# A two-filter spectral kernel: another bank plan and order for its last two stages, and another order of one step's products

## The chip, the cores and the metric

The kernel runs on one core of a Trainium2 chip. The metric is the device time of one execution in microseconds. The five engines of the core work through queues of their own: TensorE (PE in the profile; PEld is its weight loads), VectorE (DVE), ScalarE (ACT), GpSimd (POOL) and SyncE (SP), which issues most of the DMA transfers. They meet only at semaphores.

## The reference

`x` is 2048 x 1024 in bfloat16. Two filters A and B each take the two-dimensional real FFT of `x`, multiply it by a complex weight and transform it back; a sigmoid gate, one number for each row, mixes the two results.

```
x = A_x
g = _sigmoid((x * gate_w).sum(-1, keepdims=True))
X = rfft2(x)
a = irfft2(X * (A_w_r + 1j * A_w_i)).astype(bfloat16)
b = irfft2(X * (B_w_r + 1j * B_w_i)).astype(bfloat16)
return g * a + (1 - g) * b
```

Both filters read the same `x`, so the forward transform is done once.

## The kernel before

All transforms are products with constant matrices on TensorE, and the kernel keeps everything in SBUF. The numbering of the stages is that of the code.

*Stages 1 to 4* make the spectrum. After stage 1 they run as 16 **steps** `i` (`step`, line 643): stage 4 of step `i` is four matmuls (line 477) into two PSUM banks, and ScalarE copies them (line 485) into one of seven buffers in the tile XF. Step `i` uses buffer `(i + 1) % 7`, so step 14 overwrites the buffer of step 7, and step 15 that of step 8. A DMA (`swap`, line 487) writes the same data with real and imaginary parts exchanged into a second buffer in the tile MM.

*Products.* VectorE multiplies the spectrum of a step by the weights (`product`, line 493; the instruction is line 504). A step has four kinds: A0 and B0 write into the rows of the other half, A1 and B1 then write over rows that A0 and B0 read. A kinds read the direct buffer (XF), B kinds the swapped one (MM). The table `ORDER` (lines 656 to 660) gives by hand which products VectorE is handed after which step. For steps 7 and 8 each kind is cut into a first half of columns (`lo7`, `lo8`) and a second half (`up7`, `up8`). **These steps 7 and 8 are not stage 7 below.** Every dependency inside VectorE is also a semaphore wait: in this program only TensorE's instructions are never made to wait for earlier ones of the same engine.

*Stage 5* (line 600) transforms back along one axis in 32 groups of 16 matmuls, each into one of four pairs of banks, each copied by ScalarE (line 611) or now and then VectorE (line 609). Groups 1 to 15 and 0 read the products of steps 0, 1, 2 and 4 to 8, groups 16 to 31 those of steps 3 and 9 to 15. The last two groups, 30 and 31, leave banks 2 to 5.

*Stage 6* (line 748) and *stage 7* (line 777) run for 16 **row blocks** `r`. `stage6_mm(r)` is 32 small matmuls into a pair of banks, and `stage6(r)` copies the pair (line 759 on VectorE for half of block 0, line 761 on ScalarE for the rest). `stage7(r)` multiplies that by the constants DI and DJ and ends in one of three ways:

- *folded* (the `else` branch): 8 matmuls of 256 columns; ScalarE copies one bank (line 784), VectorE adds and subtracts (line 824), and GpSimd makes the output with two more (line 829);
- *half unfolded* (`HALF`): 4 matmuls of 256 and 4 of 512; ScalarE copies 256 columns, VectorE does two small additions (line 810) and two large ones that make the output (line 788). GpSimd has nothing to do;
- *wholly unfolded* (`FULL`): 8 matmuls of 512; ScalarE copies 512 columns, VectorE makes the output with line 788 alone. Block 15 ends in four additions of half the size.

Stage 7 takes banks 4 and 5 for even blocks and 2 and 3 for odd ones, so a block reuses the banks of the block two before it, and must wait until VectorE has read them. Stage 6 takes banks 0 and 1 for even blocks, 6 and 7 for odd ones. The loop (line 847) hands TensorE the stage 6 of two blocks (a "pair") ahead of the stage 7 of every odd block from 1 to 13: pair 2 and 3 before block 1, and so on. The eviction of the pair's first block goes before ScalarE's copy of this stage 7, the second one after it.

The store of a block is issued by SyncE as soon as its output is there, in the order of the blocks up to 12. Then come block 14 on ScalarE's queue, half of block 15 on SyncE's, block 13 on SyncE's, and the other half of block 15 on ScalarE's. The output tiles are reused after six blocks, GpSimd's input buffers after four folded blocks.

Of the kernel before, what the change touches and what calls it, by code (L numbers as in the profile page):

```python
# [232 lines left out]
def bass_gated_mix__spectral_gfnet__spectral_gfnet__prompt_kernel(nc, A_x, A_w_r, A_w_i, B_x, B_w_r, B_w_i, gate_w, out):  # L233
# [25 lines left out]
    def sl(t, off, dims, p0=0, np_=128, pstep=1):  # L259
        n = t.shape[1]  # L260
        return AP(t, p0 * n + off, [[n * pstep, np_]] + [list(x) for x in dims])

    def ps(col, dims):
        return AP(PS, col, [[4096, 128]] + [list(x) for x in dims])

    def bank(b):
        return ("ps", b)
# [28 lines left out]
    for _ in range(18):  # L296
        P.add("pe", lambda e: e.matmul(ps(7 * 512, [(1, 256)]), sl(CL, GRo, [(1, 128)]), sl(CL, GRo, [(1, 256)]), start=True, stop=True),
              r=["GRz"], w=[bank(7)])
# [354 lines left out]
    rest = lambda i, *a: tuple((i, k) + a for k in ("A0", "B0", "A1", "B1"))  # L653
    each = lambda *a: lambda kinds: tuple((a[0], kinds[k:k + 2]) + a[1:] for k in range(0, len(kinds), 2))
    rest = lambda *a: each(*a)("A0B0A1B1")
    ORDER = (((0, "A0"),), ((1, "A0"),), (), ((3, "A0"), (2, "A0")), ((0, "B0"), (4, "A0"), (0, "A1")))
    ORDER += tuple(((k + 1, "B0"), (k, "B1"), (k + 1, "A1")) for k in range(4))
    ORDER += tuple(((k, "A0"), (k, "B0"), (k - 1, "B1"), (k, "A1")) for k in (5, 6))
    lo7, lo8, up7, up8 = (each(k, c, 1) for c in range(2) for k in (7, 8))
    ORDER += (lo7("A0B0") + ((6, "B1"),) + lo7("A1"), lo7("B1") + lo8("A0B0A1B1") + up7("A0B0") + up8("A0B0") + up7("A1") + up8("A1") + up7("B1") + up8("B1"), rest(9))  # L660

    def products(i):
        for a in ORDER[i]:
# [70 lines left out]
    Yo = lambda k, r: (8 * k + r // 2) * RP + 264 + r % 2 * 128  # L734
    OUT = [(MM, 1024 * k) for k in range(4)] + [(XF, 6144 + 1024 * k) for k in range(2)]

    def stage6_mm(r, bs, pis):
        b0 = 6 * (r % 2)
        t6, o6, _ = RBS[r]
        for b in bs:  # L740
            for pi in pis:
                for cp in range(2):
                    n = cp * 64 + 16 * b + r
                    for h in range(2):
                        lh = sl(W, n * RP + pi, [(2, 128)], p0=64 * h, np_=64)
                        rh = sl(t6, o6 + cp * 256 + b * 32, [(128, 2), (1, 32)], p0=64 * h, np_=64)
                        o = ps((b0 + h) * 512 + pi * 256 + b * 32, [(128, 2), (1, 32)])
                        P.add("pe", lambda e, o=o, lh=lh, rh=rh, cp=cp: e.matmul(o, lh, rh, start=(cp == 0), stop=(cp == 1)),  # L748
                              r=[("Z", pi), ("RB", r)], w=[bank(b0 + h)])

    def stage6(r):
        b0 = 6 * (r % 2)
        for k in range(2 if r == 0 else 1):
            n = 4 if r == 0 else 8
            src = ps((b0 + k) * 512, [(128, n), (1, 32), (32, 4)])
            dst = sl(W, Yo(4 * k, r), [(8 * RP, n), (4, 32), (1, 4)])
            kw = dict(r=[bank(b0 + k + q) for q in range(n // 4)], a=[("Y", r)], after=[last5])
            if r == k == 0:
                P.add("dve", lambda e, s=src, d=dst: e.tensor_copy(d, s), **kw)
            else:  # L760
                P.add("act", lambda e, s=src, d=dst: e.activation(d, s, ACT.Copy), **kw)  # L761

    HALF, FULL = (2, 7, 10, 13), (5, 14, 15)
    pqc = 0

    def stage7(r):
        nonlocal pqc
        full, half = r in FULL, r in HALF
        b0 = 6 * (r - 14) if r >= 14 else 4 - 2 * (r % 2)
        ot, oo = OUT[r % NOU]  # L770
        eo = 4096 + r % 2 * 1024
        es = sl(XF, eo, [(1, 1024)]).bitcast(f32)

        def mm(col, c0, n, ri, pi, h, k, last):
            lh = sl(W, Yo((1 - h) * 4 + pi * 2 + ri, r), [(1, 128)])
            rh = sl(FT, DIo + pi * 2048 + (ri * 2 + h) * 256 + c0 * 4096, [(4096, n), (1, 256)])
            P.add("pe", lambda e: e.matmul(ps(col, [(1, n * 256)]), lh, rh, start=(k == 0), stop=(k == last)),  # L777
                  r=[("Y", r), "DI"] + ["DJ"] * (full or half), w=[bank(col // 512)])

        def ods(s, k, n):  # L780
            return sl(ot, oo + 1023 * s + 512 * (1 - 2 * s) * k, [(512 * (1 - 2 * s), n), (1 - 2 * s, 256)])

        def even(c0, n):
            P.add("act", lambda e: e.activation(es[:, :n], ps((b0 + 1) * 512 + c0, [(1, n)]), ACT.Copy), r=[bank(b0 + 1)], w=[("EO", r % 2)], after=[last5])  # L784

        def finals(k0, n, bk, t, o, keys):
            for s, op in enumerate((ALU.add, ALU.subtract)):
                P.add("dve", lambda e, s=s, op=op: e.tensor_tensor(  # L788
                    out=ods(s, k0, n), in0=ps(bk * 512, [(256, n), (1, 256)]),
                    in1=sl(t, o + 512 * k0, [(1, 512 * n)]).bitcast(f32).rearrange("p (a b) -> p a b", a=n), op=op),  # L790
                    r=keys + [bank(bk)], w=[("OU", r % NOU, s, k) for k in range(k0, k0 + n)], after=[last5])

        if full:
            for k in range(4):
                mm((b0 + 1) * 512, 0, 2, 1, k // 2, k % 2, k, 3)
            even(0, 512)
            for k0, n, bk in ((0, 2, b0),) if r < 15 else ((0, 1, b0), (1, 1, 4)):
                for k in range(4):
                    mm(bk * 512, k0, n, 0, k // 2, k % 2, k, 3)
                finals(k0, n, bk, XF, eo, [("EO", r % 2)])  # L800
        elif half:
            for e_ in (1, 0):
                for k in range(2):
                    mm((b0 + 1) * 512 + e_ * 256, 0, 1, 1, k, k ^ e_, k, 1)
            even(256, 256)
            for k in range(4):
                mm(b0 * 512, 0, 2, 0, k // 2, k % 2, k, 3)
            to = 4096 + (r % 2) * 1024
            for s, op in enumerate((ALU.add, ALU.subtract)):
                P.add("dve", lambda e, s=s, op=op: e.tensor_tensor(out=sl(MM, to + s * 512, [(1, 512)]).bitcast(f32),  # L810
                                                                   in0=ps((b0 + 1) * 512, [(1, 256)]), in1=es[:, :256], op=op),
                      r=[("EO", r % 2), bank(b0 + 1)], w=[("T", r % 2, s), ("XS", 4), ("XS", 5)])
            finals(0, 2, b0, MM, to, [("T", r % 2, 0), ("T", r % 2, 1)])
        else:
            for e_ in (1, 0):
                for ri in range(2):
                    for k in range(2):
                        mm((b0 + e_) * 512 + ri * 256, 0, 1, ri, k, k ^ e_, k, 1)
            even(0, 512)
            pk = pqc % NPQ  # L820
            pqc += 1
            pq = pk * 4096
            for s, op in enumerate((ALU.add, ALU.subtract)):
                P.add("dve", lambda e, s=s, op=op: e.tensor_tensor(out=sl(FT, pq + s * 2048, [(1, 1024)]).bitcast(f32), in0=ps(b0 * 512, [(1, 512)]),  # L824
                                                                   in1=es, op=op),
                      r=[("EO", r % 2), bank(b0)], w=[("PQ", pk, s)], after=[last5])
            pv = sl(FT, pq, [(2048, 2), (1, 1024)]).bitcast(f32).rearrange("p a (b c) -> p a b c", b=2)
            for s, op in enumerate((ALU.add, ALU.subtract)):
                P.add("pool", lambda e, s=s, op=op: e.tensor_tensor(out=ods(s, 0, 2), in0=pv[:, :, 0, :], in1=pv[:, :, 1, :], op=op),  # L829
                      r=[("PQ", pk, 0), ("PQ", pk, 1)], w=[("OU", r % NOU, s, k) for k in range(2)])  # L830
        full2 = lambda a: a.rearrange("p (a b) -> p a b", b=256)[:, ::3, :]
        ou = lambda ks: [("OU", r % NOU, s, k) for s in range(2) for k in ks]
        store = lambda eng, name, dst, src, ks: lambda: dma(eng, name, dst, src, r=ou(ks))
        if r < 15:
            return [store("act" if r == 14 else "sp", f"o{r}", outv[:, r, :], sl(ot, oo, [(1, 1024)]), (0, 1))]
        return [store("sp", "o15a", full2(outv[:, r, :]), sl(ot, oo, [(768, 2), (1, 256)]), (0,)),
                store("act", "o15b", outv[:, r, 256:768], sl(ot, oo + 256, [(1, 512)]), (1,))]
# [6 lines left out]
    stage6_mm(1, range(2, 4), (0,))  # L844
    stage6_mm(1, range(4), (1,))
    stage6(1)
    for r in range(16):
        pair = (r + 1, r + 2) if r % 2 and r < 14 else ()
        for q in pair:
            stage6_mm(q, range(4), range(2))  # L850
        for q in pair[:1]:
            stage6(q)
        late += stage7(r)
        for q in pair[1:]:
            stage6(q)
        if r < 13:
            outs.append(late.pop()())
# [63 lines left out]
```

## Time and profile before

| what | value |
|---|---|
| three runs | 121.32, 121.32, 121.65 us; median 121.32 |
| profiled execution | 121.57 us, its span 119.4 us |
| TensorE matmul busy | 110.0 us (92%) |
| TensorE weight loads busy | 88.2 us (74%) |
| VectorE busy | 97.4 us (82%) |
| ScalarE busy | 98.8 us (83%) |
| GpSimd busy | 33.9 us (28%) |
| HBM | 17.48 MB read, 4.19 MB written |

The span runs from the first to the last instruction of the program; the time of an execution has some 2 us more around it. In rows of the timeline the first number is the start in microseconds from the beginning of the span, the second the time from there to the end of the last of the instructions that the row merges; behind them stand engine, line, operation, tiles and shapes, and in brackets the idle time of the engine before the row and what ended it. Consecutive instructions of an engine overlap: a matmul of 256 columns is shown with about 0.27 us, and the next one starts about 0.11 us later. So work in a queue is counted from start to start, not by durations.

### The profile page before, as it was taken

Reading aid. Unit: us, or ns where it says so; the run is one execution under the profiler, and the core shown is the slowest. Engines: PE = TensorE matmul, PEld = TensorE weight load, DVE = VectorE, ACT = ScalarE, POOL = GpSimd, SP = SyncE. Lnnn points to the kernel's source line nnn. Section 1 sums busy time; section 2 is a strip of 40 time slices with the busy share of each in tenths; the row PEclk is TensorE's granted clock in tenths of the full one; section 3 lists DMA queues with packets and bytes.
Section 4 is the critical chain, followed back from the end, with each engine's and each line's share of the span. In section 5 each row is a group of like instructions: output and inputs, shape, how many; then the busy total and the mean of one; then the engine's idle time right before and its main releaser. Section 6 shows DMA issues by size and latency. Waiting matters only on the chain.

```text
span 119.4 us, 4238 instructions
## 1 busy us (share of the span) xinstructions
PE 110.0 (92%) x1812; PEld 88.2 (74%) x1812; DVE 97.4 (82%) x202; ACT 98.8 (83%) x119; POOL 33.9 (28%) x43
## 2 busy tenths in 40 slices
PE   6789999999999999889999999999889899999950
PEld 4566889887665766378999999999877667877420
DVE  0478998985999999999999997994537868999980
ACT  4239998999799999849999999996878968889720
POOL 1000030026664600000000000000006979789940
PEclk9999999999999999999999999999999999999999
DMA  2999999999999999844599800000000242442546
GB/s 89 314 347 412 422 379 354 350 348 349 366 362 371 361 364 363 315 150 144 128 328 401 294 4 5 0 0 5 0 5 0 96 181 88 181 176 93 206 173 236
DMA packets 17683, 26.14 MB, mean 219 GB/s; under 512 B 2113, under 2 KB 11073, under 8 KB 17665
## 3 DMA queue, kind: packets, MB, share of 16 engines
q1 hardware_dynamic: 16368, 23.00, 55.3%
q0 software_dynamic: 864, 2.36, 5.4%
q10 hardware_dynamic: 432, 0.52, 1.3%
q8 instruction: 14, 0.23, 0.8%
q14 instruction: 5, 0.03, 0.1%
HBM read 17.48 MB, written 4.19 MB: 182 GB/s over the span
## 4 chain that ended last, share of the span: by engine, by line
PE 30%; SPq 28%; POOL 12%; DMA 8%; DVE 8%; issue 6%; ACT 3%; POOLq 1%; DVEq 0%; ACTq 0%
SPq L284 28%; PE PS L600 25%; POOL MM L829 9%; DMA W<-in_B_w_i_dram 5%; DMA W<-in_A_x_dram 3%; POOL XF L829 3%; DVE W L504 3%; DVE FT L824 2%; PE PS L380 2%; DVE MM L788 2%; POOLq L860 1%; PE PS L748 1%; PE PS L777 1%; PE PS L477 1%; ACT XF L485 1%
## 5 line engine op out<-in xcount | busy, mean ns | idle before, releaser
L600 PE MATMUL PS<-CL,W 128*128 128x128 bf16 x512 | 32.4, 225 | 0.3 <-DVE W L504 0.2
L600 PEld LDWEIGHTS PS<-CL,W 128*128 128x128 bf16 x512 | 31.7, 145 | 1.3 <-DVE W L504 0.9
L829 POOL TENSOR_TENSOR MM<-FT 128x512 bf16<-128x512 f32 x14 | 17.5, 1277 | 50.9 <-DVE FT L824 50.9
L611 ACT ACTIVATE W<-PS 128x1024 bf16<-128x1024 f32 (+1 forms) x30 | 28.5, 1036 | 1.2 <-PE PS L600 1.1
L504 DVE TENSOR_TENSOR W<-XF,W 128x1024 bf16<-128x1024 bf16 (+2 forms) x36 | 22.1, 631 | 1.3 <-ACT XF L485 1.1
L504 DVE TENSOR_TENSOR W<-MM,W 128x1024 bf16<-128x1024 bf16 (+2 forms) x36 | 22.0, 636 | 0.4 <-DMA MM<-XF 0.2
L777 PE MATMUL PS<-FT,W 128*128 128x256 bf16 (+1 forms) x132 | 20.0, 302 | 0.9 <-DVE MM L788 0.4
L761 ACT ACTIVATE W<-PS 128x1024 bf16<-128x1024 f32 (+1 forms) x16 | 15.8, 994 | 3.5 <-PE PS L748 3.3
L477 PE MATMUL PS<-XF,CK 128*128 128x512 bf16 (+1 forms) x72 | 17.5, 357 | 0.8 <-ACT XF L485 0.8
L485 ACT ACTIVATE XF<-PS 128x1024 bf16<-128x1024 f32 x15 | 16.2, 1078 | 2.5 <-DVE W L504 2.1
L466 ACT ACTIVATE XF<-PS 128x1024 bf16<-128x1024 f32 x16 | 17.1, 1076 | 0.6 <-PE PS L460 0.5
L777 PEld LDWEIGHTS PS<-FT,W 128*128 128x128 bf16 x132 | 12.1, 98 | 6.7 <-DVE MM L788 0.7
L341 DVE TENSOR_TENSOR XF<-W 128x512 bf16<-128x512 bf16 (+2 forms) x34 | 11.4, 403 | 6.2 <-DMA W<-in_A_x_dram 5.9
L380 PE MATMUL PS<-MM,XF 128*128 128x256 bf16 x128 | 14.9, 273 | 1.5 <-DVE XF L341 1.4
L380 PEld LDWEIGHTS PS<-MM,XF 128*128 128x128 bf16 x128 | 12.2, 98 | 4.2 <-DVE XF L341 2.7
L391 ACT ACTIVATE FT<-PS 128x1024 bf16<-128x1024 f32 (+2 forms) x15 | 13.1, 1012 | 0.9 <-PE PS L380 0.9
L284 POOL DMA_DIRECT2D MM<-XF x18 | 9.9, 551 | 13.7 <-PE PS L477 8.1
L824 DVE TENSOR_TENSOR FT<-PS,XF 128x512 f32<-128x512 f32 x18 | 11.5, 683 | 2.3 <-ACT XF L784 2.1
L451 PEld LDWEIGHTS PS<-F,FT 128*128 128x128 bf16 x128 | 8.4, 98 | 3.1 <-ACT FT L391 0.2
L784 ACT ACTIVATE XF<-PS 128x512 f32<-128x512 f32 (+1 forms) x16 | 8.8, 547 | 1.9 <-PE PS L777 1.9
L451 PE MATMUL PS<-F,FT 128*128 128x128 bf16 x128 | 10.2, 219 | 0.0
L477 PEld LDWEIGHTS PS<-XF,CK 128*128 128x128 bf16 x72 | 4.8, 97 | 6.5 <-ACT XF L485 5.4
(63 smaller groups left out, 100.4 us busy)
## 6 DMA issues: line engine op xcount, KB each, us to landing
W<-in_A_x_dram SPq DMA_DIRECT2D x7, 512.0 KB, 7.6
out_dram<-MM SPq DMA_DIRECT2D x10, 256.0 KB, 2.7
MM<-XF POOLq DMA_DIRECT2D x18, 128.0 KB, 5.3
FT<-c_U SPq DMA_DIRECT2D x1, 2048.0 KB, 9.5
MM<-XF SPq DMA_DIRECT2D x14, 128.0 KB, 2.5
W<-in_A_w_r_dram SPq DMA_DIRECT2D x4, 256.5 KB, 6.1
W<-in_A_w_i_dram SPq DMA_DIRECT2D x4, 256.5 KB, 6.6
W<-in_B_w_r_dram SPq DMA_DIRECT2D x4, 256.5 KB, 7.0
```

The lines of the kernel that those rows point to most:

```text
L284: return P.add(eng, lambda e: e.dma_start(dst, src), dma=name, **kw)
L380: P.add("pe", lambda e, o=o, lh=lh, rh=rh, s=s: e.matmul(o, lh, rh, start=(s == 0), stop=(s == 1)), r=[("xf", c % 2, q, h, s ^ j), ("M", c ...
L451: P.add("pe", lambda e, o=o, cs=cs, j=j, t=t, rh=rh: e.matmul(o, fblock(1 + cs, j, t), rh, start=(j == 0), stop=(j == 1)), r=[("F1a" if p ...
L466: P.add("act", lambda e: e.activation(dst, src, ACT.Copy), **kw)
L477: P.add("pe", lambda e, o=o, kind=kind, pm=pm, m=m, rh=rh: e.matmul(o, sl(CK, fbo(kind, pm, m), [(1, 128)]), rh, start=(m == 0), stop=(m = ...
L485: P.add("act", lambda e: e.activation(dst, src, ACT.Copy), **kw)
L504: P.add("dve", lambda e: e.tensor_tensor(out=rows((1 - h) * 64 * RP + sw * HW), in0=sl(xt, xo + 128 * h + 64 * h0, [(0, 2), (256, 4 * ni), ...
L600: P.add("pe", lambda e, o=o, l0=l0, ab=ab: e.matmul(o, sl(W, HW * ab + l0, [(RP, 128)]), sl(CL, KIo[ab], [(1, 128)]), start=(ab == 0), sto ...
L611: P.add("act", lambda e: e.activation(dst, src, ACT.Copy), r=b, a=keys)
L761: P.add("act", lambda e, s=src, d=dst: e.activation(d, s, ACT.Copy), **kw)
L777: P.add("pe", lambda e: e.matmul(ps(col, [(1, n * 256)]), lh, rh, start=(k == 0), stop=(k == last)), r=[("Y", r), "DI"] + ["DJ"] * (full o ...
L829: P.add("pool", lambda e, s=s, op=op: e.tensor_tensor(out=ods(s, 0, 2), in0=pv[:, :, 0, :], in1=pv[:, :, 1, :], op=op), r=[("PQ", pk, 0), ...
```

## The change

Three things, all in the order of the work, its banks, and the choice of branch; the mathematics stays.

1. In the table of products, the direct product A1 of step 7's second halves is handed out right after A0 and B0 of that step, ahead of A0, B0 and A1 of step 8's second halves.
2. Stage 6 of row block 2 moves in front of the loop, in banks 4 and 5, and is copied by VectorE. The pairs then go 3 and 4 before block 2, 5 and 6 before block 4, up to 13 and 14 before block 12, and block 15 alone before block 14. Stage 6 takes banks 0 and 1 for block 0, 4 and 5 for the other even blocks, 6 and 7 for odd ones; stage 7 takes 2 and 3 for even blocks, 0 and 1 for odd ones, with 4 and 5 for block 14, and 6, 7 and 2 for block 15.
3. `HALF` becomes 2, 5, 8, 11, 13 (it was 2, 7, 10, 13), `FULL` 14 and 15 (it was 5, 14, 15). Nine blocks are folded before and after: 0, 1, 3, 4, 6, 8, 9, 11, 12 before, and 0, 1, 3, 4, 6, 7, 9, 10, 12 after.

```diff
@@ -657,7 +657,7 @@
-    ORDER += (lo7("A0B0") + ((6, "B1"),) + lo7("A1"), lo7("B1") + lo8("A0B0A1B1") + up7("A0B0") + up8("A0B0") + up7("A1") + up8("A1") + up7("B1") + up8("B1"), rest(9))
+    ORDER += (lo7("A0B0") + ((6, "B1"),) + lo7("A1"), lo7("B1") + lo8("A0B0A1B1") + up7("A0B0A1") + up8("A0B0A1") + up7("B1") + up8("B1"), rest(9))
@@ -734,8 +734,10 @@
+    S6B = lambda r: 6 if r % 2 else 4 * (r > 0)
+
     def stage6_mm(r, bs, pis):
-        b0 = 6 * (r % 2)
+        b0 = S6B(r)
@@ -749,24 +751,24 @@
     def stage6(r):
-        b0 = 6 * (r % 2)
+        b0 = S6B(r)
...
-            if r == k == 0:
+            if k == 0 and r in (0, 2):
                 P.add("dve", lambda e, s=src, d=dst: e.tensor_copy(d, s), **kw)
             else:
                 P.add("act", lambda e, s=src, d=dst: e.activation(d, s, ACT.Copy), **kw)
-    HALF, FULL = (2, 7, 10, 13), (5, 14, 15)
+    HALF, FULL = (2, 5, 8, 11, 13), (14, 15)
...
-        b0 = 6 * (r - 14) if r >= 14 else 4 - 2 * (r % 2)
+        b0 = 2 * r - 24 if r >= 14 else 2 - 2 * (r % 2)
@@ -794,7 +796,7 @@
-            for k0, n, bk in ((0, 2, b0),) if r < 15 else ((0, 1, b0), (1, 1, 4)):
+            for k0, n, bk in ((0, 2, b0),) if r < 15 else ((0, 1, b0), (1, 1, 2)):
@@ -844,8 +846,10 @@
     stage6(1)
+    stage6_mm(2, range(4), range(2))
+    stage6(2)
     for r in range(16):
-        pair = (r + 1, r + 2) if r % 2 and r < 14 else ()
+        pair = (r + 1, r + 2)[:15 - r] if r and r % 2 == 0 else ()
```

## The prediction, made before the changed kernel had run

> **What bounds the kernel now.** I read the page first, then the chain of waits, then the timeline of each engine over 48 to 54 us and from 85 us to the end.
>
> ```profile
> span 119.4 us, 4238 instructions
> ...
> PEclk9999999999999999999999999999999999999999
> ```
>
> The span is 119.4 us and the granted clock is full in every slice, so no time below has to be corrected for a clock. The chain in the middle, and the busy time of stage 5's stretch (stretch, length, busy time of TensorE, its weight loads, VectorE, ScalarE, GpSimd; clock, DMA):
>
> ```profile
> 52.43 1.03 ACT XF L485
> ```
> ```profile
> 54.42:85.58 31.16, 31.16 (x529) 31.09 (x530) 27.50 (x52) 30.07 (x34) 0.00 (x0) 1.00 0.36 124
> ```
>
> From 54.4 to 85.6 us TensorE issues stage 5 without a break; the stage goes on when one ScalarE copy (line 485, step 14's eviction) is done, and that copy starts late. So what starts it earlier moves all that follows. These rows show what it waits for (start, duration, instructions, idle time before them and its releaser; VectorE, then ScalarE's one wait of 2.1, then TensorE):
>
> ```profile
> 49.27 0.42 DVE L504 TENSOR_TENSOR W<-MM,W 128x512 bf16<-128x512 bf16 x1
> 49.73 0.43 DVE L504 TENSOR_TENSOR W<-XF,W 128x512 bf16<-128x512 bf16 x1
> ...
> 50.88 0.42 DVE L504 TENSOR_TENSOR W<-MM,W 128x512 bf16<-128x512 bf16 x1
> 51.22 0.42 DVE L504 TENSOR_TENSOR W<-XF,W 128x512 bf16<-128x512 bf16 x1
> ...
> 51.89 0.77 DVE L504 TENSOR_TENSOR W<-XF,W 128x512 bf16<-128x512 bf16 x2
> ```
> ```profile
> ACT XF L485 <- DVE W L504: 2.1, 1, 2.1
> ```
> ```profile
> 53.51 1.04 PE L477 MATMUL PS<-XF,CK 128*128 128x512 bf16 x4 [0.57 <-ACT XF L485]
> ```
>
> Step 14's copy overwrites the buffer that step 7's products read. The last reader through XF is the direct product A1 of step 7's second halves, the first of the two at 51.89, which ends at 52.31; the copy starts 0.12 later, and TensorE has stood 0.57 us for it.
>
> The end, on TensorE: a block of stage 6 is 32 matmuls of line 748; stage 7 of a row block is line 777, with 8 matmuls of 256 when folded, 4 of 256 and 4 of 512 when half unfolded, 8 of 512 when wholly unfolded:
>
> ```profile
> 86.49 0.76 PE L748 MATMUL PS<-FT,W 64*128 64x64 bf16 x40 [0.38 <-ACT W L611]
> 87.68 1.05 PE L777 MATMUL PS<-FT,W 128*128 128x256 bf16 x8 [0.43 <-DVE W L759]
> 88.66 1.11 PE L748 MATMUL PS<-FT,W 64*128 64x64 bf16 x64
> 89.70 2.35 PE L777 MATMUL PS<-FT,W 128*128 128x256 bf16 x16
> 91.98 1.11 PE L748 MATMUL PS<-FT,W 64*128 64x64 bf16 x64
> 93.02 1.48 PE L777 MATMUL PS<-FT,W 128*128 128x256 bf16 x12
> 94.94 0.61 PE L777 MATMUL PS<-FT,W 128*128 128x256 bf16 x4 [0.44 <-DVE MM L788]
> 95.48 1.11 PE L748 MATMUL PS<-FT,W 64*128 64x64 bf16 x64
> 96.52 2.77 PE L777 MATMUL PS<-FT,W 128*128 128x512 bf16 x16
> 99.23 1.11 PE L748 MATMUL PS<-F,W 64*128 64x64 bf16 x64
> ...
> 106.91 2.14 PE L777 MATMUL PS<-FT,W 128*128 128x256 bf16 x16
> 108.98 1.11 PE L748 MATMUL PS<-XF,W 64*128 64x64 bf16 x64
> 110.02 4.94 PE L777 MATMUL PS<-FT,W 128*128 128x256 bf16 x28
> ```
>
> After 95.48 TensorE hardly pauses until 114.96, where its last product is what block 15 waits for. The chain names GpSimd there, but GpSimd and VectorE both have slack:
>
> ```profile
> 90.44 4.97 POOL L829 TENSOR_TENSOR MM<-FT 128x512 bf16<-128x512 f32 x4 [48.87 <-DVE FT L824]
> 96.15 2.50 POOL L829 TENSOR_TENSOR MM<-FT 128x512 bf16<-128x512 f32 x2 [0.74 <-DVE FT L824]
> ...
> 104.87 4.98 POOL L829 TENSOR_TENSOR MM<-FT 128x512 bf16<-128x512 f32 x4 [1.26 <-DVE FT L824]
> ```
> ```profile
> 89.07 1.29 DVE L824 TENSOR_TENSOR FT<-PS,XF 128x512 f32<-128x512 f32 x2 [1.45 <-ACT XF L784]
> ...
> 93.59 1.29 DVE L788 TENSOR_TENSOR MM<-PS,MM 128x512 bf16<-128x512 f32 x2 [0.47 <-PE PS L748]
> ...
> 101.33 0.88 DVE L810 TENSOR_TENSOR MM<-PS,XF 128x256 f32<-128x256 f32 x2 [0.36 <-ACT XF L784]
> 102.31 1.29 DVE L788 TENSOR_TENSOR MM<-PS,MM 128x512 bf16<-128x512 f32 x2
> 103.51 2.70 DVE L824 TENSOR_TENSOR FT<-PS,XF 128x512 f32<-128x512 f32 x4
> ...
> 114.80 1.42 DVE L788 TENSOR_TENSOR MM<-PS,XF 128x256 bf16<-128x256 f32 x4 [0.26 <-PE PS L777]
> ```
>
> **Step 7's product order.** Today the order is 7-A0, 7-B0, 8-A0, 8-B0, 7-A1; then 7-A1 stands third. It writes rows that 7-B0 reads, so directly behind 7-B0 it must wait for it. The rows have such a pair: 49.27 to 49.73, a pitch of 0.46 instead of the usual 0.34 (50.88 to 51.22). So 7-A1 starts at 50.88 + 0.46 = 51.34, not 51.89: **0.55 us** earlier, and with it the copy, the four matmuls, the swaps that SyncE issues behind it, and stage 5. Bounds: nothing if another input is late, and 0.57, TensorE's idle time there. Without the pitch of a dependent pair it would be 0.67, cut to 0.57 by that idle time. The Trainium skill, "VectorE: DVE Perf Modes", section "The DRAIN you can't avoid", says that a semaphore between VectorE operations costs nothing extra; by that rule the copy would start 0.67 earlier. The rows here show 0.12 for a wait on the operation just before, so I do not use it.
>
> Two dependent pairs now stand close (7-B0 with 7-A1, 8-B0 with 8-A1), so VectorE's later products are 2 x 0.12 = 0.24 late, until its next long idle time at 73.97. The first to meet that is TensorE's group 16 in stage 5:
>
> ```profile
> 66.85 1.05 DVE L504 TENSOR_TENSOR W<-MM,W 128x1024 bf16<-128x1024 bf16 x2
> ```
> ```profile
> 65.94 5.07 PE L600 MATMUL PS<-CL,W 128*128 128x128 bf16 x80
> ```
>
> Those five groups run to about 70.85, 0.98 each, so the fourth, group 16, starts at 68.89, and 0.55 earlier at 68.34. Its last product ends at 67.90 + 0.24 = 68.14. It is hidden with 0.2 to spare; without that cover each 0.1 costs 0.1.
>
> **Stage 6 ahead.** Block 2's 32 matmuls go before block 0's stage 7. Two blocks take 88.66 to 89.70, 1.04 with one switch of line of 0.10, so one takes 0.47. TensorE finishes issuing block 1 at about 87.08 (40 matmuls from 86.49 at 0.0147) and waits until 87.68 for VectorE's copy: the 0.47 fits into that 0.60. The eviction of block 2 moves from ScalarE to VectorE, which the trace shows for this size in another stage:
>
> ```profile
> L609 DVE CAST W<-PS 128x1024 bf16<-128x1024 f32 x2 | 2.5, 1225 | 2.0 <-PE PS L600 2.0
> ```
>
> 1.22 us, from about 87.8 to 89.0. VectorE stands idle 1.45 us just there, to 89.07, so I take nothing; upper bound 0.2 on GpSimd's first start, which has slack. Banks: blocks 0 and 1 of stage 7 use banks that the last groups and block 0's eviction have left by 87.6, also nothing. Later blocks keep the same lead in permuted banks. So one block leaves TensorE's full stretch: **-0.47**. Block 15 alone now stands before block 14; the switches stay seven.
>
> **Fewer wholly unfolded blocks.** A full and a folded block take 96.52 to 99.23 = 2.71; a folded and a half one 89.70 to 91.98 = 2.28. Block 5 turning half gives TensorE **-0.43**. The other two half blocks only change number.
>
> **The waits for banks.** Block 4 stands still from 93.02 + 12 x 0.11 = 94.33 to 94.94, 0.61, for block 2's last additions; 0.41 of it has no cause in the trace: VectorE was ready at 93.18 and began at 93.59, and the chain has only this for it:
>
> ```profile
> 93.18 0.41 issue
> ```
>
> Blocks 11 and 12 take 106.91 to 108.98 = 2.07 where two folded ones and one switch take 2 x 0.88 + 0.10: 0.21. Together 0.81. Both are waits of the block that reuses the banks of a half block standing *second* behind a pair of stage 6 (2 and 10); block 7 stands *first* and makes none. Afterwards 2 and 8 stand first, 5 and 11 second: 2 x 0.21 = 0.42 come, 0.81 go, **-0.39**. Bounds: -0.81 if none comes, and +0.39 if each of the second ones takes 0.6. If the unexplained 0.41 returns I expect half of it on TensorE, and count 0.1 for that.
>
> Stage 7: -0.47 - 0.43 - 0.39 + 0.1 = **-1.2**, bounds -1.7 and -0.4.
>
> **Do the other engines let that through?** GpSimd: nine folded blocks at 4.97/2 = 2.49 from 90.44 give 112.8, against 114.8 now; its waits of 0.74 and 1.26 go, since VectorE gets through blocks 0, 1, 2, 3 at 89.07 + 3 x 1.29 + 2.18 = 95.1 (a half one is 103.51 - 101.33 = 2.18), before GpSimd is free at 95.41. VectorE: 1.22 + 9 x 1.29 + 5 x 2.18 + 1.29 + 1.42 = 26.4 from 87.8 ends at 114.2 at most, against 116.22 - 1.2 = 115.0. Only 0.8 to spare.
>
> **The stores.**
>
> ```profile
> out_dram<-MM ACTq DMA_DIRECT2D x1, 256.0 KB, 2.1
> ...
> out_dram<-MM SPq DMA_DIRECT2D x1, 128.0 KB, 2.2
> out_dram<-MM ACTq DMA_DIRECT2D x1, 128.0 KB, 2.7
> ```
>
> The last half store takes 2.7 since blocks 12 and 13 are stored with it; block 12's now leaves about a microsecond ahead. Between 0 and -0.5 (2.7 to 2.2); I take **-0.2**. By the Trainium skill, "DMA: Bandwidth & Descriptors", section "Anatomy of one DMA — SWDGE (gpsimd) path", some 2.0 us of a transfer is fixed and mostly the receipt of the write; an estimate by it is 2.3 alone, -0.4. These stores come from other queues, and the rows decide.
>
> **Sum.** -0.55 - 1.2 - 0.2 = -1.95. The profiled execution took 121.57, of which 119.4 is span and 2.2 lies around it: 119.62. The median shown is 121.32, 0.25 below that execution; on its scale **119.4 us**. Likeliest case alone: 118.9 to 119.9.
>
> **The rivals.** *VectorE becomes the bound.* For: 26.4 us of work in 27, and the 0.36 it idled before block 7's half; such a wait before each of five half blocks is 1.8, and it would end at 114.2 + 1.8 = 116.0, -0.2 for stage 7. Against: after blocks 0 and 1 without a pair between them, its work is ready early. With nothing from the stores, -0.75: 120.6.
> *The product order does nothing*, because the eviction is then held by something else. Against: ScalarE stands idle 2 us there for that product alone. +0.55: 119.9.
> *Slower: half blocks hold their banks.* If the 0.61 of block 4 is what a half block costs, and not a chance, it falls on blocks 4, 7, 10 and 13. With w each, stage 7 changes by -0.47 - 0.43 - 0.81 + 4w and the whole by -2.26 + 4w; it turns slower from w = 0.57 on, and at 0.70 gives 121.9. For: one of three half blocks reads 0.61 now. Against: 0.21 and 0 at the others.
>
> **How the numbers follow.** Likeliest 0.60 at 119.4; VectorE 0.20 at 120.6; order without effect 0.08 at 119.9; gains and new waits cancel 0.05 at 121.3; slower 0.07 at 121.9. A change within 0.3%, 0.36 us, can't be told from none. Faster (below 120.96) is 0.60 + 0.08 + 0.18 = 0.86; same 0.05 + 0.02 = 0.07; slower 0.07. The range 118.9 to 120.8 leaves out those two and little of the rest.
>
> **What would show it.** Line 485's late copy at 51.9 and stage 5 ending near 85.0; block 2's copy as one VectorE row of 1.22 before the first addition, and that not later than 88.6; GpSimd without idle time after its first start; TensorE's last product near 113.2; the last store landing in 2.2 to 2.5. I am wrong if GpSimd or TensorE wait for line 788 or 810 by more than 0.6 in all, or if group 16 waits for a product.

## The result, and the profile after

The changed kernel takes 119.66 us (median of four runs, 119.44 to 119.89) against 121.41 us before (four runs, 121.32 to 121.65). The ratio is 0.9853, 95% interval 0.9825 to 0.9881, so 1.75 us less. The profiled execution took 119.82 us, 1.75 less than the one before; its span is 117.6 us, 1.8 less.

Where the 1.8 us of span came from, read at three points:

| part of the span | before | after | difference |
|---|---|---|---|
| start to the first matmul of stage 7 | 87.68 | 87.50 | -0.18 |
| from there to the end of VectorE's last addition | 28.54 | 27.29 | -1.25 |
| from there to the end of the span | 3.17 | 2.82 | -0.35 |

First the product order. VectorE's timeline of the changed kernel, 49 to 52 us, then ScalarE's copy that waits for step 7's A1, then TensorE's rows for step 15's matmuls and the group before them:

```profile
49.27 0.43 DVE L504 TENSOR_TENSOR W<-XF,W 128x512 bf16<-128x512 bf16 x1 [0.58 <-DMA W<-in_B_w_i_dram]
...
51.23 0.42 DVE L504 TENSOR_TENSOR W<-MM,W 128x512 bf16<-128x512 bf16 x1
51.68 0.77 DVE L504 TENSOR_TENSOR W<-XF,W 128x512 bf16<-128x512 bf16 x2
```
```profile
52.23 1.02 ACT L485 ACTIVATE XF<-PS 128x1024 bf16<-128x1024 f32 x1 [1.92 <-PE PS L600]
```
```profile
52.12 1.19 PE L600 MATMUL PS<-CL,W 128*128 128x128 bf16 x16
53.31 1.04 PE L477 MATMUL PS<-XF,CK 128*128 128x512 bf16 x4
```

Step 7's A1 now starts 0.45 behind B0, the pitch of a dependent pair, and two places earlier. The copy follows A1's start by 0.55, as before (51.89 to 52.43, 0.54), so A1 still releases it, though its row names a TensorE group that ended about then. It ends at 53.25 and TensorE's own group at 53.31, where step 15's matmuls start: the two now meet. But the first product of step 8, which waits for the last weights, starts at 49.27 and not at 48.93 as before. Counted from that product, step 15's matmuls come 4.04 us later, against 4.58 before: 0.54 less. Counted from the start of the span only 0.20 is left, because the weights came later in this execution.

Then TensorE in stages 6 and 7:

```profile
86.31 1.23 PE L750 MATMUL PS<-FT,W 64*128 64x64 bf16 x72 [0.38 <-ACT W L611]
87.50 1.92 PE L779 MATMUL PS<-FT,W 128*128 128x256 bf16 x16
...
97.03 2.17 PE L779 MATMUL PS<-FT,W 128*128 128x256 bf16 x16
99.13 1.11 PE L750 MATMUL PS<-F,W 64*128 64x64 bf16 x64
...
106.81 2.57 PE L779 MATMUL PS<-FT,W 128*128 128x256 bf16 x16
109.31 0.64 PE L750 MATMUL PS<-XF,W 64*128 64x64 bf16 x32
```

Block 2's matmuls (72 in the first row instead of 40) fill the time before 87.50 that was idle. Two waits for banks are left: blocks 6 and 7 take 99.13 - 97.03 = 2.10 where two folded blocks with a switch take 1.86, and blocks 12 and 13 take 2.50 where a folded and a half one took 2.28. That is 0.46, against 0.81 before. VectorE and GpSimd:

```profile
87.60 1.22 DVE L761 CAST W<-PS 128x1024 bf16<-128x1024 f32 x1 [0.16 <-PE PS L750]
88.89 2.49 DVE L826 TENSOR_TENSOR FT<-PS,XF 128x512 f32<-128x512 f32 x4
91.45 0.88 DVE L812 TENSOR_TENSOR MM<-PS,XF 128x256 f32<-128x256 f32 x2
92.45 1.29 DVE L790 TENSOR_TENSOR MM<-PS,MM 128x512 bf16<-128x512 f32 x2
...
113.37 1.42 DVE L790 TENSOR_TENSOR MM<-PS,XF 128x256 bf16<-128x256 f32 x4 [0.26 <-PE PS L779]
```
```profile
90.26 7.44 POOL L831 TENSOR_TENSOR MM<-FT 128x512 bf16<-128x512 f32 x6 [48.75 <-DVE FT L826]
...
109.97 2.52 POOL L831 TENSOR_TENSOR MM<-FT 128x512 bf16<-128x512 f32 x2
```

The copy of block 2 takes 1.22 us and ends just as the first addition can start. GpSimd has no idle time from 90.26 to 112.49. Line 790 of block 2 follows at once: the wait of 0.41 us without a cause, which stood there before, is gone. The last half store takes less, 2.3 us from issue to landing where it took 2.7:

```profile
out_dram<-MM ACTq DMA_DIRECT2D x1, 128.0 KB, 2.3
```

### The profile page after: what moved, and what is told of

It is laid out like the page before. It is cut to its first block, busy times and chain, and to the rows that moved or that the text cites. A ratio compares the mean times of both kernels' runs of the same rounds, so it can differ in the third digit from the quotient of the medians.

```text
span 117.6 us, 4239 instructions
## 1 busy us (share of the span) xinstructions
PE 110.4 (94%) x1812; PEld 88.5 (75%) x1812; DVE 99.7 (85%) x205; ACT 97.7 (83%) x118; POOL 33.7 (29%) x43
## 4 chain that ended last, share of the span: by engine, by line
PE 55%; SPq 28%; DMA 6%; DVE 3%; issue 2%; ACT 2%; DVEq 0%; POOL 0%; POOLq 0%
SPq L284 28%; PE PS L600 27%; PE PS L779 14%; PE PS L750 7%; DMA W<-in_B_w_i_dram 6%; PE PS L297 3%; PE PS L380 2%; DVE W L504 1%; ACT XF L786 1%; DVE MM L790 1%; PE PS L477 1%; PE PS L559 1%; ACT W L611 1%; PE PS L578 1%; DVE XF L790 0%
## 5 line engine op out<-in xcount | busy, mean ns | idle before, releaser
L611 ACT ACTIVATE W<-PS 128x1024 bf16<-128x1024 f32 (+1 forms) x30 | 28.6, 1034 | 1.2 <-PE PS L600 1.1
L763 ACT ACTIVATE W<-PS 128x1024 bf16<-128x1024 f32 (+1 forms) x15 | 14.8, 992 | 3.9 <-PE PS L750 3.9
```

The costliest lines, as they stand in the source:

```text
L611: P.add("act", lambda e: e.activation(dst, src, ACT.Copy), r=b, a=keys)
```

## The experiments

The kernels e1 to e12 were run in three comparisons, e1 to e4, e5 to e8 and e9 to e12, each of five rounds and beside runs of the kernel before, to which the ratio refers. The median of the kernel before was 121.63, 121.47 and 121.70 us in them, so ratios compare better than medians across the three. The columns are: median; ratio to before with its 95% interval; from the first product of step 8 to step 15's matmuls (P); from stage 7's first matmul to the end of VectorE's last addition (S); from there to the end of the span (T). The last three are from the profile of each run.

| kernel | median us | ratio | P | S | T |
|---|---|---|---|---|---|
| before | 121.41 | 1 | 4.58 | 28.54 | 3.17 |
| changed | 119.66 | 0.9853 (0.9825 to 0.9881) | 4.04 | 27.29 | 2.82 |
| e1 order only | 120.89 | 0.9942 (0.9921 to 0.9963) | 4.05 | 28.55 | 3.12 |
| e2 old order | 120.35 | 0.9908 (0.9873 to 0.9943) | 4.59 | 27.29 | 2.82 |
| e3 old sets | 120.16 | 0.9897 (0.9858 to 0.9936) | 4.05 | 27.47 | 3.16 |
| e4 sets only | 120.93 | 0.9946 (0.9921 to 0.9972) | 4.59 | 28.13 | 2.82 |
| e5 first places | 119.74 | 0.9854 (0.9826 to 0.9882) | 4.05 | 26.83 | 3.72 |
| e6 copy on ScalarE | 120.28 | 0.9900 (0.9870 to 0.9929) | 4.04 | 28.17 | 2.83 |
| e7 store 13 first | 118.86 | 0.9784 (0.9757 to 0.9811) | 4.05 | 27.29 | 2.47 |
| e8 step 7 fills the wait | 119.29 | 0.9823 (0.9792 to 0.9854) | 3.86 | 27.29 | 2.82 |
| e9 changed again | 119.68 | 0.9824 (0.9795 to 0.9854) | 4.04 | 27.29 | 2.81 |
| e10 store 13 first again | 119.20 | 0.9792 (0.9769 to 0.9815) | 4.03 | 27.29 | 2.51 |
| e11 first places, stores in order | 118.27 | 0.9724 (0.9692 to 0.9756) | 4.04 | 26.83 | 2.27 |
| e12 e11 with e8's order | 118.40 | 0.9729 (0.9706 to 0.9751) | 3.84 | 26.83 | 2.27 |

P, S and T repeat to 0.05 us between kernels that share the part. The medians don't; most likely because the first product of step 8, which waits for the last weights, starts anywhere from 48.62 (e1) to 49.98 us (e2), but only the profiled executions show that start.

**The parts alone.** The order on the old stages 6 and 7 (e1), the old order on the new ones (e2), the old sets in the new schedule (e3) and the new sets in the old one (e4):

```diff
 # e1 = before with the + line, e2 = changed with the - line
-... + up7("A0B0") + up8("A0B0") + up7("A1") + up8("A1") + up7("B1") + up8("B1"), ...
+... + up7("A0B0A1") + up8("A0B0A1") + up7("B1") + up8("B1"), ...
 # e3 = changed with the upper line, e4 = before with the lower one
-HALF, FULL = (2, 7, 10, 13), (5, 14, 15)
+HALF, FULL = (2, 5, 8, 11, 13), (14, 15)
```

> The kernel before with the new order of step 7's products alone. Theory: line 485's late copy starts 0.55 earlier counted from the first product that waits for the last weights (2.96 after it, 3.50 before), and stage 5 follows 1 to 1: 0.5 us less than before, ratio 0.996. The changed kernel's profile showed only 0.2 because its last weights landed 0.34 later. Rival: the gain is only the 0.2 that the changed kernel's profile shows, since TensorE's own queue (two groups of stage 5 in front) takes over as the bound: ratio 0.998.

> The changed kernel with step 7's old product order: stage 6, its banks and the choice of branches alone. Theory: from stage 7's first matmul to VectorE's last addition 27.3 us (28.5 before, 27.3 in the changed kernel), the last store's landing 0.3 shorter, so 1.6 less than before, ratio 0.987, and 0.2 to 0.5 above the changed kernel. Rival: the order of the products does nothing, and this one is as fast as the changed kernel, ratio 0.985.

> The changed kernel with the old sets (half 2, 7, 10, 13; full 5, 14, 15): stage 6 ahead, banks and product order stay. Theory: TensorE has 0.43 more in block 5, and of the waits for banks only one of 0.22 stays (block 9, behind 7, which now stands second) where the changed kernel has two: 0.2 above the changed kernel, ratio to before 0.987. Rival (half blocks hold up VectorE, which has only 0.8 to spare): with one half block less this is as fast as the changed kernel or faster, ratio 0.985 or below.

> The kernel before with the new sets alone (half 2, 5, 8, 11, 13; full 14, 15). Theory: TensorE has 0.43 less; halves 2 and 8 stand second behind a pair, so blocks 4 and 10 wait for banks; block 4's wait is 0.2 or, if the 0.41 without a cause comes again, 0.6. 0.4 (with it) to 0.8 (without it) less than before, ratio 0.993 to 0.997. Rival: a half block costs VectorE and the banks more than it saves, same time as before or above, ratio 1.000 or more.

*e1* gives 0.58% less (0.37 to 0.79%), that is 0.45 to 0.96 us: the 0.54 of P lies inside, the rival's 0.2 does not. Its profile has the same 4.05 between the first product of step 8 and step 15's matmuls:

```profile
48.62 0.43 DVE L504 TENSOR_TENSOR W<-XF,W 128x512 bf16<-128x512 bf16 x1 [0.24 <-DMA W<-in_B_w_i_dram]
```
```profile
52.67 1.04 PE L477 MATMUL PS<-XF,CK 128*128 128x512 bf16 x4
```

TensorE has no idle time left before these matmuls.

*e2* has the new S and T with the old P. Its median is 1.28 less than before and not 1.6, but its profile starts step 8's products 1.05 us later than the one before; counted from there the span is 1.6 shorter (68.8 against 70.5). The rival, that the order does nothing, falls with P: 4.59 against 4.04.

*e3*: S rises by 0.18 where 0.2 was expected: 0.43 for the full block, less the 0.25 by which its waits for banks are shorter (0.21 in all against 0.46). The wait that stays is that of block 9, behind half block 7, which stands second in this schedule:

```profile
100.41 2.14 PE L779 MATMUL PS<-FT,W 128*128 128x256 bf16 x16
102.48 0.64 PE L750 MATMUL PS<-F,W 64*128 64x64 bf16 x32
```

2.07 instead of 1.86. Against the kernel before, which has the same sets, S is 1.07 less: 0.60 of it are waits for banks (0.81 to 0.21), and the 0.47 that remain are the block whose stage 6 moved ahead. Its median is 0.5 above the changed kernel's and not 0.2; the expectation missed T, which is 0.34 longer: the sets, and not the schedule, shorten the end. *e4* says the same from the other side: T is 2.82 with the new sets in the old schedule. With the old sets GpSimd's last output is done 1.5 us ahead of VectorE's (e3), with the new ones 2.3 us (e4), and block 12's store, which waits for it, stands before those of blocks 13 and 15.

*e4* itself: S falls by 0.41, T by 0.35, and the median by 0.70 us, as expected with the 0.41 coming again. It does come again, at the same instruction:

```profile
92.58 0.87 DVE L810 TENSOR_TENSOR MM<-PS,XF 128x256 f32<-128x256 f32 x2
93.93 1.29 DVE L788 TENSOR_TENSOR MM<-PS,MM 128x512 bf16<-128x512 f32 x2 [0.47 <-DVE MM L810]
```

**The waits for banks.** The half blocks moved to places that stand first behind a pair:

```diff
-HALF, FULL = (2, 5, 8, 11, 13), (14, 15)
+HALF, FULL = (2, 6, 8, 12, 13), (14, 15)
```

> The changed kernel with the half blocks at 2, 6, 8, 12 and 13: all but 13 stand first behind a pair of stage 6, and none of the first four makes the block two behind it wait. Theory (a half block that stands second makes the next user of its banks wait 0.22): both waits go, no stall of TensorE in stage 7, 0.44 less than the changed kernel, ratio to before 0.982. Rival: the wait belongs to every half block whose VectorE work queues behind a folded one's, whatever its place; it stays, ratio 0.985.

S falls by 0.46 to 26.83, and the two-block rows that could hold a wait hold none:

```profile
93.59 1.92 PE L779 MATMUL PS<-FT,W 128*128 128x256 bf16 x16
95.44 0.64 PE L750 MATMUL PS<-FT,W 64*128 64x64 bf16 x32
...
103.13 1.92 PE L779 MATMUL PS<-FT,W 128*128 128x256 bf16 x16
104.98 1.11 PE L750 MATMUL PS<-XF,W 64*128 64x64 bf16 x64
```

Both take 1.85, two folded blocks with nothing between. So the rule of the places holds for these sets, and its rival falls. The rows show where the difference arises. Block 5 of the changed kernel stands second (its matmuls are the later half of the first row below); block 6 of e5 stands first (the earlier half of the third row):

```profile
93.71 2.35 PE L779 MATMUL PS<-FT,W 128*128 128x256 bf16 x16
97.24 1.29 DVE L790 TENSOR_TENSOR XF<-PS,MM 128x512 bf16<-128x512 f32 x2
```
```profile
96.48 2.35 PE L779 MATMUL PS<-FT,W 128*128 128x256 bf16 x16
98.52 1.29 DVE L790 TENSOR_TENSOR MM<-PS,MM 128x512 bf16<-128x512 f32 x2
```

From a half block's first matmul TensorE comes back to its second bank after some 3.76 us (the folded neighbour 0.88, the block itself 1.40, a pair 1.04, half a folded block 0.44). VectorE's last addition ends 3.94 us after block 5's first matmul (93.71 + 0.88 = 94.59 to 98.53), too late, and 3.33 after block 6's (96.48 to 99.81), in time. Every half block but 13 shows this in every profile but e6's: 3.3 to 3.4 in first place, 3.9 in second, and 4.3 where the 0.41 without a cause comes on top. That the folded block directly in front delays VectorE in second place is the likely reason; it was not tested alone.

But the time does not follow (0.9854): T grows from 2.82 to 3.72, so that S and T together are 0.44 longer than in the changed kernel. Block 12 is now half unfolded and its output is there at 109.35 (VectorE's row below), but SyncE issues the stores in the order of the blocks, and block 11, now GpSimd's last (to 112.38), holds up the one behind it. Block 11's store (the second of the first row, issued up to 112.74) and the three behind it (blocks 12, half of 15, 13) leave SyncE within 2.5 us (e5, start and length from the first issue to the last):

```profile
108.06 1.29 DVE L790 TENSOR_TENSOR MM<-PS,MM 128x512 bf16<-128x512 f32 x2
```
```profile
107.40 4.98 POOL L831 TENSOR_TENSOR XF<-FT 128x512 bf16<-128x512 f32 x4
```
```profile
109.93 2.81 SPq L284 DMA_DIRECT2D out_dram<-XF  x2
112.78 2.07 SPq L284 DMA_DIRECT2D out_dram<-MM  x3
```

**The copy of block 2.** On ScalarE instead of VectorE:

```diff
-            if k == 0 and r in (0, 2):
+            if r == k == 0:
```

> The changed kernel with block 2's copy on ScalarE and not on VectorE. Theory: ScalarE's copies of blocks 1 and 2 now both stand ahead of block 0's copy in stage 7, which starts 0.90 later; VectorE's first additions and GpSimd's start come 0.9 later, GpSimd has 1 us to spare and VectorE 0.8, so 0.2 to 0.6 slower than the changed kernel, ratio 0.987 to 0.990. Rival: the start has slack enough for either engine, same as the changed kernel, ratio 0.985.

```profile
86.44 2.43 ACT L763 ACTIVATE W<-PS 128x512 bf16<-128x512 f32 x3 [0.53 <-PE PS L750]
88.74 1.11 ACT L786 ACTIVATE XF<-PS 128x512 f32<-128x512 f32 x2
```
```profile
89.46 2.48 DVE L826 TENSOR_TENSOR FT<-PS,XF 128x512 f32<-128x512 f32 x4 [2.36 <-ACT XF L786]
91.86 0.87 DVE L812 TENSOR_TENSOR MM<-PS,XF 128x256 f32<-128x256 f32 x2
93.20 1.29 DVE L790 TENSOR_TENSOR MM<-PS,MM 128x512 bf16<-128x512 f32 x2 [0.47 <-DVE MM L812]
```
```profile
90.04 2.67 PE L779 MATMUL PS<-FT,W 128*128 128x256 bf16 x16
92.65 1.11 PE L750 MATMUL PS<-FT,W 64*128 64x64 bf16 x64
93.69 0.61 PE L779 MATMUL PS<-FT,W 128*128 128x256 bf16 x4
94.54 2.23 PE L779 MATMUL PS<-FT,W 128*128 128x256 bf16 x12 [0.25 <-DVE MM L790]
96.71 0.64 PE L750 MATMUL PS<-FT,W 64*128 64x64 bf16 x32
```

The three copies of blocks 0 to 2 now run one after the other on ScalarE. VectorE's first addition comes 2.31 us after stage 7's first matmul and not 1.39, 0.92 later, and S is 0.88 longer. TensorE meets it in the first half blocks: 90.04 to 92.65 is 2.61 instead of 2.28, waiting for line 826 to leave a bank, and 93.69 to 96.71 is 3.02 instead of 2.28, waiting for lines 790 and 826. Blocks 6 and 7 then take 1.91 instead of 2.10, so 0.33 + 0.74 - 0.19 = 0.88. So VectorE's 0.8 us of slack does not exist for a late start. GpSimd's was not tested apart: it ends 0.9 later, but so does VectorE, 2.25 us behind it (2.30 in the changed kernel). The time is 0.5% above that of the changed kernel's first timing and 0.8% above the control's (0.9900 against 0.9853 and 0.9824); by S and T it is 0.9 us, more than the 0.2 to 0.6 expected. The 0.41 without a cause is here too, and part of the 0.88 may be its: block 4's wait of 0.41 before 94.54 starts there. How much is the copy's alone was not separated.

**The stores.** Block 13's store before the first half of block 15's:

```diff
-    outs += [late[k]() for k in (1, 2, 0, 3)]
+    outs += [late[k]() for k in (1, 0, 2, 3)]
```

> The changed kernel with block 13's store issued ahead of block 15's first half on SyncE's queue. Its output is there 2 us before SyncE issues it, behind the wait for block 15. Theory: two half stores are left for the end, the last one lands in 2.0 and not 2.3: 0.3 less than the changed kernel, ratio 0.983. Rival: the 2.3 are the fixed time of a store, not its neighbours: no change, ratio 0.985.

> The changed kernel once more, on the chip of the three runs that follow. Theory: the part from stage 7's first matmul to VectorE's last addition is 27.3 again, and what differs between runs is when the last weights land (48.4 to 49.9 in the profiles so far), which moves the end 1 to 1: ratio to before 0.985, within 0.003.

> Block 13's store first, again, beside the control. Theory: 0.3 less than the control, all of it behind VectorE's last addition (2.5 from there to the span's end against 2.8); the 0.7 that the first run of this kernel was below the changed kernel was half earlier weights. Rival: the full 0.7 is the store's, ratio to the control 0.994.

T is 2.47 and 2.51 in the two runs, against 2.82 and 2.81: 0.3 less. The last store in the first of them:

```profile
out_dram<-MM ACTq DMA_DIRECT2D x1, 128.0 KB, 2.0
```

So its 2.3 were not a fixed time. The first run's median lay 0.8 below the changed kernel's first timing; beside the control it is 0.48 (119.20 against 119.68), and the control, the same program as the changed kernel, reads 0.9824 with an interval that holds 0.9853. More than 0.3 is not shown.

**The wait for the last weights.** Two of step 7's products moved into it:

```diff
-... lo7("B1") + lo8("A0B0A1B1") + up7("A0B0A1") + up8("A0B0A1") + ...
+... lo7("B1") + up7("A0B0") + lo8("A0B0A1B1") + up7("A1") + up8("A0B0A1") + ...
```

> The changed kernel with A0 and B0 of step 7's second halves ahead of step 8's first halves, in the 0.6 us in which VectorE stands for the last weights. Theory: line 485's late copy starts 0.7 earlier, but TensorE's two groups in front of step 15's matmuls now set the start of stage 5 (the gap before these matmuls is 0.13 in the changed kernel), and they wait for step 8's first halves, 0.1 later: no gain, 0 to 0.1 slower than the changed kernel, ratio 0.985 to 0.986. Rival: the copy still sets it, 0.6 less, ratio 0.980.

```profile
51.20 1.02 ACT L485 ACTIVATE XF<-PS 128x1024 bf16<-128x1024 f32 x1 [1.14 <-DVE W L504]
```
```profile
51.88 1.19 PE L600 MATMUL PS<-CL,W 128*128 128x128 bf16 x16
52.91 1.03 PE L477 MATMUL PS<-XF,CK 128*128 128x512 bf16 x4
```

The copy ends at 52.22, and step 15's matmuls start only at 52.91, straight behind TensorE's own group: the copy no longer sets stage 5's start. P is 3.86 here, but that is no gain. The first product of step 8 now runs straight behind step 7's (48.38, 48.71, 49.05), and the last weights had landed at 48.49:

```profile
49.05 0.42 DVE L504 TENSOR_TENSOR W<-XF,W 128x512 bf16<-128x512 bf16 x1
```

Counted from that landing, step 15's matmuls come after 4.42 us here and after 4.40 in e12, against 4.14 in the changed kernel and in e11. The median was 0.4 below the changed kernel's first timing, which looked like a gain; e12 was to settle that.

**Both improvements.** The sets of e5, with SyncE's last stores in the order in which the outputs are made, and the same with e8's order:

```diff
-        if r < 13:
+        if r < 11:
             outs.append(late.pop()())
-    outs += [late[k]() for k in (1, 2, 0, 3)]
+    outs += [late[k]() for k in (1, 2, 0, 3, 4, 5)]
```

> Half blocks at 2, 6, 8, 12, 13 and SyncE's last stores in the order in which their outputs are made: 12, 13, 11, then half of 15. Theory: TensorE's 0.46 of waits for banks go as before with these sets, and now reach the end, since block 12's store no longer stands behind block 11's: span from stage 7's first matmul 29.4 against 30.1 in the control, 0.7 less than the control, ratio to before 0.979. Rival: the stores of the last 3 us share the same transfer engines, and the gain in stage 7 is again lost there: at most 0.3 below the control.

> The kernel with both, and besides A0 and B0 of step 7's second halves ahead of step 8's first halves. Theory: TensorE's two groups in front of step 15's matmuls set the start of stage 5, so counted from the last weights' landing step 15's matmuls start no earlier (4.1 after it) and up to 0.3 later where the weights land early: 0 to 0.2 slower than the kernel with both. Rival: 0.3 faster, as the first run with this order was against the changed kernel's first timing.

S is 26.83 and T 2.27, so S + T is 29.10 against 30.10 in the control, 1.0 less where 0.7 was expected: besides the 0.46 of the banks, T itself is 0.54 shorter. The median is 1.4 less than the control's, at 118.27 us; the 0.4 beyond S + T is not accounted for. Its last half store lands in 1.8:

```profile
out_dram<-MM ACTq DMA_DIRECT2D x1, 128.0 KB, 1.8
```

*e12* is not faster: 0.9729 against 0.9724, and 118.40 against 118.27. So the gain that e8 seemed to have is not shown. e11 beats both kernels of this study, 3.4 us below the kernel before by the medians of its own comparison (121.70 and 118.27).

## Why the prediction was right

The prediction gave 119.4 us, 118.9 to 120.8; 119.66 was measured. Step by step:

- **Step 7's product order, -0.55.** The mechanism and its size hold: P is 0.54 shorter in every kernel with the new order, and the pitch of the dependent pair is 0.45 where 0.46 was taken. By the rule of the Trainium skill, "VectorE: DVE Perf Modes", section "The DRAIN you can't avoid", that a semaphore between VectorE operations costs nothing, it would have been 0.67; these rows disagree by 0.12 for each wait on the operation just before. What the prediction did not have is that the last weights' landing, which it took as given, differs by more than a microsecond between profiled executions, and moves what follows with it as long as VectorE waits for it: P stays within 4.03 and 4.05 in the kernels with this order, e8 and e12 apart. In the profiled execution it took back 0.34, which is why the start of stage 7 moved by 0.18 alone. The signs that came 0.3 late, the copy at 52.23 for 51.9, stage 5's end at 85.40 for 85.0 and the first addition at 88.89 for 88.6, are this shift.
- **Group 16 hidden with 0.2 to spare.** Held: stage 5 runs without a break after the change, and from step 15's matmuls to stage 7's first it takes 34.19 us after 34.17 before; in e1 it is 34.17 too.
- **Stage 6 ahead, -0.47, and VectorE's copy for nothing.** Held: block 2's matmuls end before 87.50, e3 against the kernel before leaves 0.47 for the block, and the copy took the 1.22 us predicted. e6 shows what the choice of VectorE is worth: with the copy on ScalarE S is up to 0.9 longer.
- **Block 5 half, -0.43.** Held: e3's S is 0.18 longer, 0.43 less the 0.25 that its waits are shorter.
- **The waits for banks, -0.39, and 0.1 for the unexplained 0.41.** -0.35 was measured (0.81 to 0.46). The rule of the first and second place was read off two waits and one half block without any, with no reason given; it stood four tests: the changed kernel (5 and 11 second, two waits), e3 (7 second, one), e4 (2 and 8 second, two), and e5 (none of the first four second, none). The waits are VectorE's lateness, 3.94 us where TensorE leaves it 3.76. The 0.41 did not come again, so the 0.1 for it was too much.
- **Stage 7 in all, -1.2:** -1.25.
- **"Only 0.8 to spare" on VectorE.** This reading was wrong, though nothing hung on it here. A sum of VectorE's work says that it could end by 114.2; but each late addition also holds a bank that TensorE needs two blocks on, so e6's late start of 0.92 made S 0.88 longer. The slower rival (half blocks that hold their banks) named that chain; at the waits of 0.2 that the changed kernel has, it does not decide. The other rival, VectorE as the bound, did not come either: it idles at most 0.17 before a half block's additions, and its last additions still wait for TensorE (0.26 before 113.37).
- **The stores, -0.2.** The mechanism was right and the size too small: -0.35, and another -0.3 was to be had from their order. The estimate of 2.3 for the last store by the Trainium skill, "DMA: Bandwidth & Descriptors", section "Anatomy of one DMA — SWDGE (gpsimd) path", agrees with the 2.3 of the changed kernel, but the 2.7 before lies above it, and 2.0 in e7 and 1.8 in e11 lie below it: for these queues the measurement decides.

The sum was -1.95, and -1.8 of span was measured: the weights' later landing (+0.34) and the better stage 7 and stores (-0.2) make the difference. So part of the closeness is luck: by P, S and T together the change is worth 2.14 us, and beside the control it reads 2.02; the first timing's 1.75 lies below the forecast 1.95, though the parts lie above it.

## What to carry to other kernels

Compare profiles from an event that both share and neither changes, here the first product after the last weights: read from the start of the span, the largest single term of this change looked like 0.2 instead of 0.54. Slack that is a sum of an engine's work can't be trusted where another engine waits for the banks that it reads; look instead at who reuses the bank, and how soon. When a faster stage does not shorten the time, look at the issue order of the last stores: a queue that waits for the slowest output holds up those that are ready.

## What the runs showed of the hardware that was not expected

The 0.41 us in which VectorE was ready and did not start stand before the same instruction (block 2's first line 788 or 790) in the four profiled kernels in which ScalarE copies block 2: before, e1, e4 and e6. In the other ten, the changed kernel among them, VectorE executes that copy itself, and the row follows after 0.1 us. So it goes with which engine makes that copy, and with what this changes in VectorE's sequence and times, and not with chance; what it is stays open, and no run was made for it.

The last weights land anywhere from 48.49 (e8) to 49.89 us (e2) in these profiles, in programs whose loads are the same; a first product that waits for them starts 0.1 later. In e8, e10 and e12 they land before VectorE comes to it. That spread of 1.4 us is larger than most of the parts measured here.
